# Folding the wide value products: four f32 products with a 0/1 matrix in place of four transposes and a VectorE sum

## The chip, the cores and the metric

The kernel runs on one core of one Trainium2 chip. The metric is the device time of one execution in microseconds (us); lower is better. The kernel before has a median of 193.93 us over 3 runs.

## The reference

One decode step of attention over a sliding window, gated by a small MLP. The inputs are bf16, with 32 heads of 128, a window of the last W = 4096 positions, and x of 512 values:

```
xn = _layernorm(x)
q  = (xn @ wq).reshape(32 heads, 128)
k  = k_cache[:, :, Sk - W:, :]          # 32 x 4096 x 128
v  = v_cache[:, :, Sk - W:, :]          # 32 x 4096 x 128
p  = softmax(einsum("hd,hkd->hk", q, k) * 128 ** -0.5)
s  = einsum("hk,hkd->hd", p, v).reshape(4096) @ wo
g  = silu(mlp(xn))                      # the weights w2, w3 and w4 are used
out = x + s * g
```

K and V of the window are 33.5 MB each. That is most of the 79 MB that one execution reads.

## The kernel before, in words

The 32 heads go in `NG` = 8 groups of `G` = 4 heads. A group's K is one tile of 128 partitions: 32 partitions belong to each head, and each partition holds 128 positions of 128 values (32 KB). The group's V lies in the same way. `load` issues every such load on SyncE's queue, in the order of the program. K tiles come from `k_pool` (3 buffers) and V tiles from `v_pool` (2 buffers), so a load waits on SyncE's queue until the last reader of its buffer is through. The wq load and two small loads of x are issued on ScalarE's queue.

The program begins with constants, the layer norm of x, q and the MLP. The order of instructions on the engines there is left to a planner. Then comes a loop of 10 stages, `for s in range(NG + LAG)` at L531, whose order on TensorE (PE), VectorE (DVE) and ScalarE (ACT) is as written. Stage s works on three groups at once:

- Group s: the scores. VectorE takes half of the positions or more (`k_vector`: a product, L321, and a sum, L323). For the others, TensorE transposes K (`k_turn`, L339), ScalarE copies the result to `kt` (L342), and TensorE multiplies with q (`k_scores`, L350).
- Group s - 1: the softmax. `sm_max` is its maximum on VectorE. `sm_turn` and `sm_exp` bring the maximum of each head to all partitions (L372 to L384) and take the exponentials on ScalarE (L388).
- Group h = s - 2 (`LAG` = 2): the value products. `v_wide` (L427) multiplies four columns of probabilities for four heads at once (16 columns, `pT`) with 512 values of V. So each product holds 4 x 4 blocks of which only those whose column fits the position are wanted, and four row groups at partitions 0, 32, 64 and 96 share the sum. ScalarE copies the result to `ov_sb` (L433), 128 rows of 4 x 128 f32 values.

The wanted rows of `ov_sb` are folded by three steps, one stage later in stages 3 to 6. For block j the wanted row of head a is row 32 r + 4 j + a, for r from 0 to 3, and the four row groups and the four blocks are to be summed:

- `v_turn` transposes the four 128 x 128 blocks on TensorE into one PSUM tile `ot_ps`. Each block is written 4 columns further left than 128 j, so that the wanted columns of all blocks fall in with each other (L444).
- `v_add` sums 16 values for each of the 4 heads on VectorE (L450) and gives `oT`, 128 x 4.
- `v_out` scales `oT` with the inverse denominator `rden`. In groups 0 to 2 that is four ScalarE operations (L475), from group 3 on one VectorE operation (L471).

`ps_misc` is a pool of one PSUM buffer. The tile `ot_ps` of groups 0 to 6, the denominators (`sm_den`, L394, an f32 product of a 128 x 128 matrix of ones with 4 columns, read by `sm_rden` at L399), the transposed maximum, the tile `mb_ps` and the tiles of `ox_pick` follow each other in it. Each waits until the one before has been read. The last group, 7, uses a buffer of `ps_tr`, and its `oT` is a PSUM tile that takes further products (`v_part`) behind the sum.

Groups 0 to 3 are folded in stages 3 to 6, behind `sm_exp` and before `v_wide`. Group 4 is folded early in stage 7, group 5 at the end of stage 7, group 6 in stage 8 and group 7 in stage 9. In stages 8 and 9 the output products with wo (`y_wide`, `y_head`) and a few products on zeros (`warm`) stand between these steps.

Tiles lie in SBUF pool by pool as the program opens them: K, `kt` and `prod`, then constants, small tiles, the softmax's tiles (`sm_pool`), and last the weights, whose place V's tiles take from stage 2 on.

Of the kernel before, what the change touches and what calls it, by code (L numbers as in the profile page):

```python
# [8 lines left out]
P = 128  # L9
BF16 = mybir.dt.bfloat16  # L10
FP32 = mybir.dt.float32
ACT = mybir.ActivationFunctionType
ALU = mybir.AluOpType
AX = mybir.AxisListType
# [4 lines left out]
G = 4  # L19
# [7 lines left out]
def kernel(  # L27
# [14 lines left out]
    nc = tc.nc  # L42
# [20 lines left out]
    const = ctx.enter_context(tc.tile_pool(name="const", bufs=1))  # L63
    small = ctx.enter_context(tc.tile_pool(name="small", bufs=1))
    ps_misc = ctx.enter_context(tc.tile_pool(name="ps_misc", bufs=1, space=PSUM))
    ps_tr = ctx.enter_context(tc.tile_pool(name="ps_tr", bufs=3, space=PSUM))
# [3 lines left out]
    sm_pool = ctx.enter_context(tc.tile_pool(name="sm", bufs=3))  # L70
# [4 lines left out]
    def load(dst, src):  # L75
# [9 lines left out]
                        in_=A_wq.rearrange("(a b c) n -> b a (c n)", a=4, c=KC))  # L85
# [19 lines left out]
    ident_f = const.tile([P, P], FP32, name="ident_f")  # L105
# [16 lines left out]
    nc.vector.memset(neg_half[:], -0.5)  # L122

    masks = {}

# [75 lines left out]
    for b in range(2):  # L203
        zeros(qr[b][:])
        for c in range(KC):
            wc = wq_sb[:, c, :].rearrange("p (g a d) -> p g a d", a=G, d=Dh)
            for a in range(G):
                nc.tensor.matmul(qr[b][32 * a:32 * a + 1], lhsT=xq_bf[:, c:c + 1], rhs=wc[:, 4 * b:4 * b + 4, a, :],  # L208
                                 start=False, stop=(c == KC - 1), skip_group_check=True)
    nc.scalar.copy(out=q_row[:, 0:4, 0, :], in_=qr[0][:])  # L210
    nc.vector.tensor_copy(out=q_row[:, 4:8, 0, :], in_=qr[1][:])  # L211
    for b in range(2):
        qb_ps = ps_tr.tile([P, 4, Dh], FP32, tag="pt", name="qb_ps")
        nc.tensor.matmul(qb_ps[:], lhsT=sel[:].rearrange("k b a -> k (b a)"), rhs=q_row[:, 4 * b:4 * b + 4, 0, :],
                         start=True, stop=True)
        nc.scalar.copy(out=q_bc[:, 4 * b:4 * b + 4, :], in_=qb_ps[:])
    for b in range(2):
# [5 lines left out]
        for t in range(2):  # L223
            rows = slice(64 * t, 64 * t + 64)
            nc.scalar.copy(out=q_pair[rows, 4 * b:4 * b + 4, :, G * t:G * t + G].rearrange("p g l a -> p g a l"),
                           in_=qt_ps[rows].bitcast(BF16).rearrange("p g (a m l) -> p g a m l", a=G, l=2)[:, :, :, 0, :])
# [4 lines left out]
    for j in range(KC):  # L231
        for c in range(KC):
            nc.tensor.matmul(hs_ps[:, j:j + 1], lhsT=w2_sb[:, c, j::4],
                             rhs=shifted_bf[:, c:c + 1], start=(c == 0), stop=(c == KC - 1))
# [33 lines left out]
    for i, (col, w) in enumerate(terms):  # L268
        r = 32 * (i % 4)
        nc.tensor.matmul(hr_ps[r:r + 1].rearrange("r j n -> r (j n)"), lhsT=col, rhs=w, start=False,  # L270
                         stop=(i >= len(terms) - 4), skip_group_check=True)
# [25 lines left out]
                            op=ALU.max)  # L297
# [136 lines left out]

    def v_turn(g):
        s = st[g]
        if g == NG - 1:
            ot_ps = ps_tr.tile([P, 4 * P], FP32, tag="pt", name="ot_ps")
        else:
            ot_ps = ps_misc.tile([P, 4 * P], FP32, tag="misc", name="ot_ps")  # L440
        s["ot"] = ot_ps
        step = P - 4
        for j in range(4):
            nc.tensor.transpose(ot_ps[:, step * j:step * j + P], s["ov_sb"][:, j, :], ident_f[:])  # L444

    def v_add(g):
        s = st[g]
        if g < NG - 1:
            s["oT"] = sm_pool.tile([P, G], FP32, tag="oT", name="oT")
        nc.vector.tensor_reduce(out=s["oT"][:], in_=s["ot"][:].rearrange("p (x m) -> p m x", m=32)[:, 0:G, :],  # L450
                                axis=AX.X, op=ALU.add)

# [72 lines left out]
    NG = H // G  # L525
# [5 lines left out]
    for s in range(NG + LAG):  # L531
# [22 lines left out]
        if s < NG:  # L554
# [11 lines left out]
            if s == 7:  # L566
                v_turn(h - 1)
                v_add(h - 1)
                v_out(h - 1)
            elif s > 1:  # L570
                sm_den(s - 2)
                sm_rden(s - 2)
            elif s == 1:
                sm_max(0)
# [14 lines left out]
            if s == 7:  # L589
                k_vector(s, kn, 2)  # L590
                v_wide(h, v)
                sm_exp(s - 1)
                v_turn(h)
                y_open()
                k_vector(s, kn, 3)
                v_add(h)
                v_out(h)
                ox_spread(1)
                sm_max(s)
                continue  # L600
            if s > 0:
                sm_exp(s - 1)
            if h > 0:
                v_turn(h - 1)
# [3 lines left out]
            if h > 0:  # L608
                v_add(h - 1)
                v_out(h - 1)  # L610
# [74 lines left out]
```

## Time and profile before

| What | Value |
|---|---|
| Median of 3 runs | 193.93 us (193.26 to 193.96) |
| Span of the profiled execution | 191.2 us |
| The profiled execution's own time | not listed beside its span; the median less the span is 2.7 us |
| Busy: PE, DVE, ACT, POOL | 116.4, 150.9, 89.2, 2.3 us |
| DMA | 79.02 MB, mean 413 GB/s over the span |
| Mean granted TensorE clock | 0.720 |
| Four fold transposes of one group (L444) | 0.66 us at granted clock 1.0, 1.05 to 1.11 us at 0.5 |
| The fold's sum (L450) | 8 operations, median 0.215 us |
| Scaling (L471, L475) | 0.16 us each (5), 0.29 us each (12) |

The profile is one execution, and its times count from the span's start. PE is the matmuls, PEld the weight loads. A digit row cuts the span in 40 equal slices of 4.8 us, and each digit is the busy share in tenths. The chain of waits is followed back from the last instruction, at each step to what released it; where it names a DMA, the time runs from the issue of the load to its landing, and waiting in the queue behind earlier loads is part of it. In the windows each line has the stretch, its length, the busy time of the engines with their instruction counts, the granted clock, the mean busy share of the 16 DMA engines and GB/s.

### The profile page before, as it was taken

How to read it: one execution, taken by the hardware profiler on the slowest of the kernel's cores; microseconds unless marked ns; L12 is line 12 of the kernel's file. 1: busy time of each engine (PE TensorE's matmuls, PEld its weight loads, DVE VectorE, ACT ScalarE, POOL GpSimd, SP SyncE). 2: the span in 40 equal slices, each digit the busy share in tenths (PEclk: the TensorE clock that was granted, in tenths of full speed). 3: DMA queues.
4: the chain of work that ended last, by engine and by line, in shares of the span. 5: the costliest groups of instructions: out<-in, count | busy, mean ns of one | idle time of the engine just before them, and what ended most of it. 6: DMA issues, size and time to landing. Idle time of an engine off the chain costs nothing.

```text
span 191.2 us, 2839 instructions
## 1 busy us (share of the span) xinstructions
PE 116.4 (61%) x1159; PEld 74.2 (39%) x1159; DVE 150.9 (79%) x175; ACT 89.2 (47%) x191; POOL 2.3 (1%) x11
## 2 busy tenths in 40 slices
PE   1653754989825368256845772680888189739762
PEld 0430222767614334143334441540763077313322
DVE  1660159979999999999999999999999999980111
ACT  2001370888794076427464564542475148733120
POOL 2110000000000000000000000000000000000000
PEclk9999695555755557955695588557567858975998
DMA  6999999999999999999999999999999998999990
GB/s 211 447 430 404 431 418 439 439 439 437 432 434 439 432 429 432 432 439 432 422 432 432 418 422 418 452 439 435 439 432 434 435 432 372 471 425 405 420 371 32
DMA packets 4572, 79.02 MB, mean 413 GB/s; under 512 B 624, under 2 KB 1232, under 8 KB 1488
## 3 DMA queue, kind: packets, MB, share of 16 engines
q1 hardware_dynamic: 4264, 74.65, 91.6%
q10 hardware_dynamic: 296, 4.20, 5.1%
q8 instruction: 9, 0.15, 0.3%
q14 instruction: 3, 0.02, 0.0%
HBM read 78.84 MB, written 0.00 MB: 412 GB/s over the span
## 4 chain that ended last, share of the span: by engine, by line
DVE 46%; DMA 43%; PE 5%; ACT 3%; issue 1%; SPq 1%; ACTq 0%; DVEq 0%
DMA kv<-in_A_k_cache_dram 31%; DVE S L323 28%; DVE prod L321 15%; DMA kv<-in_A_v_cache_dram 10%; ACT kt L342 3%; DMA x_bf<-in_A_x_dram 2%; PE pt L339 2%; PE ov L427 1%; DVE m L366 1%; DVE S L364 1%; SPq L76 1%; PE sT L350 1%; DVE mx L374 1%; PE oT L461 1%; PE ot_ps L444 0%
## 5 line engine op out<-in xcount | busy, mean ns | idle before, releaser
L323 DVE TENSOR_REDUCE S<-prod 128x20 f32<-128x2560 bf16 (+1 forms) x32 | 86.0, 2686 | 1.1
L342 ACT COPY kt<-pt 128x1024 bf16<-128x1024 bf16 x52 | 51.2, 1013 | 40.4 <-PE pt L339 38.7
L339 PE MATMUL pt<-ident_f,kv 128*128 128x128 f32 x208 | 46.7, 376 | 10.8 <-DMA kv<-in_A_k_cache_dram 10.8
L321 DVE TENSOR_TENSOR prod<-kv,q_bc 128x2560 bf16<-128x2560 bf16 (+1 forms) x32 | 45.4, 1418 | 3.9 <-DMA kv<-in_A_k_cache_dram 3.7
L339 PEld LDWEIGHTS pt<-ident_f,kv 128*128 128x128 f32 x208 | 34.2, 196 | 14.4 <-DMA kv<-in_A_k_cache_dram 10.5
L350 PE MATMUL sT<-q_pair,kt 128*128 128x8 bf16 x416 | 19.4, 170 | 15.7 <-ACT kt L342 15.5
L350 PEld LDWEIGHTS <-kt 128*128 128x128 bf16 x416 | 16.4, 104 | 26.8 <-ACT kt L342 25.8
L427 PE MATMUL ov<-kv,pT 128*16 128x512 bf16 x248 | 22.0, 515 | 1.4 <-DMA kv<-in_A_v_cache_dram 1.4
L388 ACT ACTIVATE pT<-S,mb 128x128 bf16<-128x128 f32 x32 | 13.9, 573 | 0.3
L372 PE MATMUL mt_ps<-ident_f,m 128*1 128x128 f32 x8 | 2.9, 359 | 17.4 <-DVE rden L399 16.9
L433 ACT COPY ov_sb<-ov 128x512 f32<-128x512 f32 x8 | 4.7, 586 | 17.1 <-PE ov L427 17.1
L427 PEld LDWEIGHTS <-pT 128*16 128x16 bf16 x248 | 6.9, 109 | 13.2 <-issue 11.4
L359 ACT ACTIVATE own<-sT,par 128x48 f32<-128x48 f32 (+1 forms) x32 | 7.5, 356 | 3.7 <-PE sT L350 3.7
L444 PE MATMUL ot_ps<-ident_f,ov_sb 128*128 128x128 f32 x32 | 7.1, 359 | 2.9 <-ACT mb L384 1.9
L211 DVE CAST q_row<-qr_ps 128x512 bf16<-128x512 f32 x1 | 0.7, 692 | 9.9 <-PE qr_ps L208 9.9
L388 ACT ACTIVATION_READ_ACCUMULATOR pT<-S,mb 128x1 f32 x32 | 8.3, 258 | 0.0
L372 PEld LDWEIGHTS mt_ps<-ident_f,m 128*1 128x1 f32 x8 | 0.6, 80 | 17.9 <-DVE rden L399 17.2
L399 DVE RECIPROCAL rden<-den_ps 128x4 f32<-128x4 f32 x8 | 1.4, 175 | 7.0 <-PE den_ps L394 7.0
L381 PE MATMUL mb_ps<-md,par_t 5*128 5x4 f32 x16 | 3.9, 311 | 4.1 <-DVE md L376 4.1
L255 ACT ACTIVATE a_row<-a_ps 128x384 bf16<-128x384 f32 x1 | 0.5, 491 | 12.0 <-remote 12.0
L444 PEld LDWEIGHTS ot_ps<-ident_f,ov_sb 128*128 128x128 f32 x32 | 4.5, 178 | 3.9 <-ACT mb L384 2.3
L208 PE MATMUL qr_ps<-wq_sb,xq_bf 128*1 128x512 bf16 x32 | 3.1, 566 | 3.7 <-DMA wq_sb<-in_A_wq_dram 3.7
(122 smaller groups left out, 81.6 us busy)
## 6 DMA issues: line engine op xcount, KB each, us to landing
kv<-in_A_k_cache_dram SPq DMA_DIRECT2D x7, 4096.0 KB, 31.3
kv<-in_A_v_cache_dram SPq DMA_DIRECT2D x7, 4096.0 KB, 30.6
wq_sb<-in_A_wq_dram ACTq DMA_DIRECT2D x1, 4096.0 KB, 17.6
kv<-in_A_k_cache_dram SPq DMA_DIRECT2D x2, 2048.0 KB, 27.4
wo<-in_A_wo_dram SPq DMA_DIRECT2D x1, 2048.0 KB
kv<-in_A_v_cache_dram SPq DMA_DIRECT2D x1, 2048.0 KB
kv<-in_A_v_cache_dram SPq DMA_DIRECT2D x2, 1024.0 KB, 17.6
w_sb<-in_B_w_dram SPq DMA_DIRECT2D x1, 1376.0 KB, 9.1
```

What stands on the lines that cost most here:

```text
L321: nc.vector.tensor_tensor(out=prod[:, 0:m, :], in0=kn[:, rows, :], in1=q_bc[:, g:g + 1, :].to_broadcast([P, m, Dh]), op=ALU.mult)
L323: nc.vector.tensor_reduce(out=st[g]["S"][:, rows], in_=prod[:, 0:m, :], axis=AX.X, op=ALU.add)
L339: nc.tensor.transpose(pt[:, i, :], kn[:, c:c + 2, :].rearrange("p c d -> p (c d)").bitcast(FP32), ident_f[:])
L342: nc.scalar.copy(out=kts[b][:, 0:n, :], in_=pt[:, 0:n, :].bitcast(BF16))
L350: nc.tensor.matmul(st[g]["sT"][:, c:c + 2, :].rearrange("p c a -> p (c a)"), lhsT=kt[:, i, l::2], rhs=q_pair[:, g, l, :], start=(l == 0), ...
L359: nc.scalar.mul(s["own"][:, 0:m, a], s["sT"][:, 0:m, a], par[:, a:a + 1])
L372: nc.tensor.transpose(mt_ps[:], s["m1"][:], ident_f[:])
L381: nc.tensor.matmul(mb_ps[:], lhsT=par_t[:].rearrange("k b a -> k (b a)"), rhs=md[:], start=True, stop=True)
L388: nc.scalar.activation(out=s["pT"][:, :, a], in_=s["S"][:], func=ACT.Exp, scale=scale, bias=mb[:, a:a + 1], accum_out=s["sum"][:, a:a + 1])
L427: nc.tensor.matmul(ov[r:r + 4 * G], lhsT=s["pT"][:, c:c + 4, :].rearrange("p i a -> p (i a)"), rhs=v[:, c:c + 4, :], start=(i < 4), stop=( ...
L433: nc.scalar.copy(out=s["ov_sb"][:], in_=ov[:])
L444: nc.tensor.transpose(ot_ps[:, step * j:step * j + P], s["ov_sb"][:, j, :], ident_f[:])
```

## The change

A constant `fold` (128 x 4 x 4, f32) is made of the identity by one VectorE maximum: for block j and head a, it has ones in the four rows 32 r + 4 j + a. In groups 0 to 6, `v_turn` multiplies each block of `ov_sb`, as the stationary operand, with that block's 4 columns of `fold`, and the four products add up in one PSUM tile `oT` of 128 x 4 in the pool `ps_misc`. `v_add` does nothing there any more, and `v_out` reads `oT` from PSUM where it read SBUF. Group 7 is left as it was. The SBUF tiles `oT` of `sm_pool` (three buffers of 16 bytes per partition, each in a slot of 32) go away, and `fold` takes 64 bytes per partition.

```diff
+    fold = const.tile([P, 4, G], FP32, name="fold")
+    nc.vector.tensor_reduce(out=fold[:].rearrange("p j a -> p (j a)"),
+                            in_=ident_f[:].rearrange("p (r m) -> p m r", m=32)[:, 0:4 * G, :],
+                            axis=AX.X, op=ALU.max)
...
     def v_turn(g):
         s = st[g]
-        if g == NG - 1:
-            ot_ps = ps_tr.tile([P, 4 * P], FP32, tag="pt", name="ot_ps")
-        else:
-            ot_ps = ps_misc.tile([P, 4 * P], FP32, tag="misc", name="ot_ps")
+        if g < NG - 1:
+            s["oT"] = ps_misc.tile([P, G], FP32, tag="misc", name="oT")
+            for j in range(4):
+                nc.tensor.matmul(s["oT"][:], lhsT=s["ov_sb"][:, j, :], rhs=fold[:, j, :], start=(j == 0),
+                                 stop=(j == 3))
+            return
+        ot_ps = ps_tr.tile([P, 4 * P], FP32, tag="pt", name="ot_ps")
         s["ot"] = ot_ps
         step = P - 4
         for j in range(4):
...
     def v_add(g):
         s = st[g]
         if g < NG - 1:
-            s["oT"] = sm_pool.tile([P, G], FP32, tag="oT", name="oT")
+            return
         nc.vector.tensor_reduce(out=s["oT"][:], in_=s["ot"][:].rearrange("p (x m) -> p m x", m=32)[:, 0:G, :],
                                 axis=AX.X, op=ALU.add)
```

## The prediction

> **What bounds the kernel now.** I read the page's totals and slices first, then the chain of waits, then the DMA issues, and last the windows, to see whether the chain tells the truth.
>
> ```profile
> span 191.2 us, 2839 instructions
> ...
> DVE  1660159979999999999999999999999999980111
> ...
> DMA  6999999999999999999999999999999998999990
> ```
>
> Two resources are full from about 30 to 165 us: VectorE and the DMA engines. Only DMA stays full from 2 to 186 us. Which one sets the end decides everything, because the change takes work from VectorE and adds none to DMA.
>
> ```profile
> 128.66 0.13 DVE oT L450
> 128.79 1.41 DVE prod L321
> 130.20 0.02 SPq L76
> 130.22 0.03 issue
> 130.25 23.26 DMA kv<-in_A_k_cache_dram
> 153.52 0.04 issue
> 153.56 1.13 PE pt L339 x4
> ...
> 167.79 18.54 DMA kv<-in_A_v_cache_dram
> 186.33 0.05 issue
> 186.38 0.97 PE oT L461 x32
> ```
>
> The chain names VectorE up to 130 us, with the reduction that the change removes (L450) on it. But it jumps into loads of 23.26 and 18.54 us. A 4096 KB load (4.19 MB) takes 9.7 us at the 432 GB/s of the windows below. So the K load issued at 130.25 lay 23.26 - 9.7 = 13.6 us behind earlier loads. An issue a little earlier or later lands at the same time.
>
> ```profile
> kv<-in_A_k_cache_dram SPq DMA_DIRECT2D x1, 4096.0 KB, 22.1
> ```
>
> ```profile
> 60.45:78.65 18.20, 10.28 (x109) 6.55 (x109) 17.98 (x13) 9.56 (x21) 0.00 (x0) 0.64 1.01 433
> 78.65:96.87 18.22, 10.62 (x96) 6.74 (x97) 18.02 (x14) 8.00 (x22) 0.00 (x0) 0.63 1.00 431
> ...
> 153.50:170.30 16.80, 12.92 (x143) 9.33 (x143) 16.06 (x21) 11.19 (x22) 0.00 (x0) 0.80 1.01 435
> 170.30:186.40 16.10, 11.85 (x116) 4.85 (x117) 2.63 (x13) 3.67 (x12) 0.00 (x0) 0.82 0.96 402
> 186.40:191.20 4.80, 1.33 (x48) 1.05 (x48) 0.75 (x3) 0.00 (x0) 0.00 (x0) 0.85 0.09 32
> ```
>
> The first line is the DMA issue at 112.03 us, the shortest wait of any full K or V load: 22.1 - 9.7 = 12.4 us of queue ahead of it. The others range up to 38.3 us. The windows (columns: PE, PEld, DVE, ACT, POOL busy, granted clock, DMA share, GB/s) show a DMA share of 1.0 in stages where VectorE is busy 99% too, and 0.96 in the stage after 170 us where VectorE has almost nothing to do (2.63 of 16.1 us). The page counts 79.02 MB; at 432 GB/s that is 183 us of the 191.2. The rest is the start, and the 4.8 us behind the last landing at 186.4 us. The kernel is bound by its loads.
>
> The sum is made against a time. Span 191.2 us, median of the runs 193.93, so about 2.7 us lie around the span (2.1 to 2.8 over the three runs).
>
> **The change part by part.** *VectorE loses* seven reductions of 0.215 us (the tile's row gives 215/215/233 ns for all eight; the eighth stays): 1.5 us busy. On the chain each shows as 0.13 us, since its start overlaps the tail of the operation before it; around 147.4 and 157.5 us the step to the next start is 0.25 us. So between 0.9 and 1.75 us leave VectorE's order. In stages 3 to 6 the next K load is issued up to that much earlier in all, into a queue at least 12.4 us deep: worth 0.
>
> *VectorE gains* the reduction that makes `fold`, 64 values in and 16 out per partition: between 0.215 us (L450, also 64 values) and 0.37 us (L296, 128 values). It needs only the identity matrix, ready at 1.8 us, and VectorE stands idle 3.4 us before 4.7 us and 9.87 us before 23.1 us. Even in the worst place, ahead of the q chain, 0.37 us is covered: TensorE waits until 19.9 us for wq. Without that cover it would cost 0.37 us.
>
> *TensorE.* A 0/1 product in f32 is not in the trace, but the denominator's product has the same stationary size and the same 4 columns, and it runs as two weight loads and two matmuls (x16 for eight calls).
>
> ```profile
> 88.92 1.11 PE L444 MATMUL ot_ps<-ident_f,ov_sb 128*128 128x128 f32 x4 [0.25 <-ACT mb L384]
> ```
>
> ```profile
> 173.22 0.50 PEld L394 LDWEIGHTS den_ps<-sum,ones_f 128*128 128x128 f32 x2 [0.85 <-ACT mb L384]
> 173.23 0.59 PE L394 MATMUL den_ps<-sum,ones_f 128*128 128x4 f32 x2
> 178.40 0.39 PE L394 MATMUL den_ps<-sum,ones_f 128*128 128x4 f32 x2
> ```
>
> Four transposes last 1.11 us at the granted clock of 0.5 and 0.66 us at 1.0. A pair of denominator passes takes 0.59 us at 0.5; one lasts 0.376, so a pass follows the last after 0.21 us. At 1.0 I take 0.36 to 0.39 us for a pair and 0.25 for one: 0.11 us apart. Eight passes are then 7 x 0.21 + 0.38 = 1.85 us or 7 x 0.11 + 0.25 = 1.02 us. That is +0.74 us in groups 0, 1, 2 and 4 (clock 0.5) and +0.36 us in groups 3, 5 and 6 (1.0), about 4 us of TensorE over the kernel. Bounds for one group: nothing (if the passes overlap fully) to twice the transposes, +1.1 us. In stages 3 to 6 this delays the wide products, and so the release of a V buffer and a V load's issue, by 0.4 to 1.1 us; those loads take 25.9 to 32.3 us to land, 9.7 of them transfer, so it is hidden by 16 us.
>
> The rows have an f32 weight load at 186 to 190 ns at the full clock and up to 333 at half, 0.11 or 0.21 us from the next. The Trainium skill ("TensorE: Matmul & The Clock Gate", LDWEIGHTS) gives a load its column count over 1.2 in ns, 107 for 128 columns, whatever the clock. By it, an estimate, eight passes would end after some 1.1 us in every group, so the groups at half clock would pay nothing and stage 7 would not slip. The trace's 0.21 us contradicts it at half clock; either way the time comes to 193.9, as the cost is hidden.
>
> Stage 7 is tightest: there the chain runs on TensorE from 153.5 to 166.5 us, and the last V load is issued behind its wide product. Group 4's +0.74 us moves that issue (166.8 to 167.8 us) to at most 168.9. V's last 4.19 MB and the last 0.52 MB of wo rows need 10.9 us and end at about 186.4, so they start at about 175.5: 6 us or more are left. In stage 8, group 6 ends 0.36 us later, but its 0.25 us step on VectorE is gone. The warm products behind it end at 180.5, the first V piece lets TensorE go on at 181.5, and the second at 183.9: a delay of 0.36 to 1.1 us is taken up there. Behind 186.4 us nothing is changed.
>
> *Waits.* The product now stays in the one `misc` bank until the output scaling has read it. In groups 0 to 2 that is ScalarE (four operations, 0.85 us from 94.09), so the next user, the denominator's product at 96.10, waits for ScalarE in place of VectorE. It stands behind scores that wait for a `kt` copy, which ScalarE issues after those four operations: nothing added. From group 3 VectorE's scaling reads PSUM; its row is 161/164/164 ns, group 7's from PSUM among them: 0.
>
> Sum: 193.93 - 0 (VectorE) + 0 (TensorE) = **193.9 us**.
>
> **The rivals.** *Loads into shifted tiles get dearer (slower).* `fold` adds 64 bytes per partition ahead of the pools of weights and V; `oT` frees three slots of 32. Laid out in order, those tiles start 32 bytes lower, so no longer at a multiple of 64. K tiles lie in front and keep their place. The moved tiles take some 42 MB (V 33.6, wq and w2 to w4 7.5, wo 1.0), or 97.5 us of transfer. One extra 256-byte piece per 32 KB row would be 1/128: 0.76 us, 194.7. One extra 32-byte step for each 256 bytes would be 1/8: 12 us, 206. It decides (over 0.97 us) from 1% per moved byte, and there is no queue to hide it. For it: DMA has no slack. Against it: K tiles and V tiles already lie differently against 256 bytes, and they stream alike.
>
> ```profile
> q1 hardware_dynamic: 126, 3.64, 99.8%
> ```
>
> ```profile
> q1 hardware_dynamic: 116, 3.44, 99.6%
> ```
>
> First a window inside the K load that lands at 153.5 (144.5 to 153 us), then one inside the V load that lands at 143.8 (135 to 143 us): 3.64 / (8.5 x 16 x 0.998) and 3.44 / (8 x 16 x 0.996), 26.8 and 27.0 GB/s per engine. No load of size here starts 32 bytes off, so the trace doesn't exclude it. The Trainium skill ("DMA: Bandwidth & Descriptors", How a descriptor splits into AXI transactions) says that a descriptor whose start is off a multiple of 256 bytes pays for one more transaction: the 0.76 us case. K against V shows no such price. Chance 0.27, most of it between 194.9 and 198.
>
> *VectorE is the bound after all (faster).* The chain's 46% speaks for it, the queue of 12 us against it. It gives 193.93 less 0.9 to 1.75: 192.2 to 193.0. Chance 0.05.
>
> *The last V load starves (slower).* If the DMA queue ran dry before it, stage 7's +0.74 and group 6's +0.36 us would come through: 195.0. It needs a delay of over 6 us. Chance 0.04.
>
> **How the numbers follow.** The forecast has 0.64; its own range is 193.2 to 194.5. About 0.5% (0.97 us) is what a measurement of this kernel can tell from no change; the three runs spread over 0.70 us. Slower by more: 0.23 of the first rival and 0.04 of the last, 0.27. Faster by more: 0.05, and 0.02 for spread. Within: 0.66. The range takes the forecast, the edge of the faster case and the shifted-tile case up to 2% per moved byte and some more: 193.0 to 197.0.
>
> **What would show it.** Right: DMA still 9 in every slice to the end, 32 KB rows at the same pace, the last V landing near 186.4, L450 once, some 16 TensorE passes for each of groups 0 to 6 (8 loads, 8 matmuls) in 1.0 to 1.9 us, and a tail of 4.8 us. Wrong: V windows below K windows in GB/s (tiles), an earlier last landing (VectorE), a gap in DMA before the last V load (starving), or TensorE at a lower granted clock behind 186 us.

## The result and the profile after

The changed kernel takes 195.44 us (median of 4 runs, 195.36 to 195.51) against 193.63 us for the kernel before in the same job: 1.0102 times, 95% interval 1.0089 to 1.0116. It is slower by 1.8 us, inside the range, and not where the forecast put it. Two small costs on the loads make the difference, both side effects of where the change put bytes and instructions: one 16 KB instruction fetch that now comes ahead of the last V rows, and tiles that no longer start at a multiple of 256 bytes.

The profiled run took 195.36 us with a span of 193.6. First the lines of its page that answer to those of before:

```profile
span 193.6 us, 2890 instructions
...
PE 124.7 (64%) x1187; PEld 82.4 (43%) x1187; DVE 150.3 (78%) x169; ACT 89.0 (46%) x191; POOL 2.3 (1%) x11
...
DVE  1660069979999999999999999998999986970111
...
DMA  6999999999999999999999999999999998998960
```

TensorE has 28 more weight loads and 28 more matmuls (1187 against 1159): four more of each in every one of the seven groups. DMA still stands at 8 or 9 until shortly before the end. The end has moved, though. In the chain of waits (start, length, what):

```profile
130.49 23.37 DMA kv<-in_A_k_cache_dram
...
170.35 18.14 DMA kv<-in_A_v_cache_dram
188.49 0.05 issue
188.54 0.97 PE oT L469 x32
```

The last V piece lands at 188.49 us, where before it was 186.33: 2.16 us later. Its issue came 2.56 us later, at 170.35, and that is not the reason: in e3 below, which has no new fold, it is issued at 170.35 too and lands at 187.04:

```profile
170.35 16.70 DMA kv<-in_A_v_cache_dram
```

The windows (PE, PEld, DVE, ACT, POOL busy, granted clock, DMA share, GB/s):

```profile
60.45:78.65 18.20, 9.98 (x109) 6.53 (x109) 17.96 (x14) 9.79 (x21) 0.00 (x0) 0.65 1.01 431
...
173.00:188.50 15.50, 12.24 (x118) 5.05 (x118) 1.61 (x9) 3.57 (x12) 0.00 (x0) 0.80 0.88 359
188.50:193.60 5.10, 1.58 (x48) 1.16 (x48) 0.74 (x3) 0.00 (x0) 0.00 (x0) 0.59 0.01 4
```

In mid-kernel the DMA engines are as busy and move a little less, 431 GB/s where it was 433. In the stage up to V's landing they are busy 0.88 on average, where it was 0.96: most have finished while the chain still waits for V, and the packet records below show that one of the 16 is late. The answer to which transfer made it late is in the DMA queues between 5 and 186 us, first of the kernel before, then of the changed one (queue, packets, MB, share):

```profile
q8 instruction: 8, 0.13, 0.3%
```

```profile
q8 instruction: 9, 0.15, 0.3%
```

Queue q8 brings 16 KB of instructions at a time. Nine such packets stand in each trace. The ninth came at 187.05 us before, behind V's last row, and at 185.58 us after, ahead of it. The packet records show its price: the fetch took its engine 1.10 us, and the V row of 8 KB behind it 0.77 us where such a row takes 0.31. That is 1.10 and another 0.46 us on one engine. Its last V rows ended at 187.44, 187.75 and 188.06 us; every other V row had ended by 186.49, 1.57 us earlier.

### The profile page after: what moved, and what is told of

It is laid out like the page before. It is cut to its first block, busy times and chain, and to the rows that moved or that the text cites. A ratio compares the mean times of both kernels' runs of the same rounds, so it can differ in the third digit from the quotient of the medians.

```text
span 193.6 us, 2890 instructions
## 1 busy us (share of the span) xinstructions
PE 124.7 (64%) x1187; PEld 82.4 (43%) x1187; DVE 150.3 (78%) x169; ACT 89.0 (46%) x191; POOL 2.3 (1%) x11
## 4 chain that ended last, share of the span: by engine, by line
DVE 43%; DMA 42%; PE 10%; ACT 2%; issue 1%; SPq 1%; ACTq 0%; DVEq 0%
DMA kv<-in_A_k_cache_dram 31%; DVE S L328 26%; DVE prod L326 13%; DMA kv<-in_A_v_cache_dram 9%; PE pt L344 3%; PE ov L432 3%; DMA x_bf<-in_A_x_dram 2%; PE oT L445 2%; ACT kt L347 2%; PE sT L355 1%; DVE m L371 1%; DVE S L369 1%; SPq L76 1%; DVE mx L379 1%; PE oT L469 1%
## 5 line engine op out<-in xcount | busy, mean ns | idle before, releaser
L344 PE MATMUL pt<-ident_f,kv 128*128 128x128 f32 x208 | 48.8, 389 | 9.8 <-DMA kv<-in_A_k_cache_dram 9.8
L344 PEld LDWEIGHTS pt<-ident_f,kv 128*128 128x128 f32 x208 | 35.8, 203 | 13.1 <-DMA kv<-in_A_k_cache_dram 9.4
L432 PE MATMUL ov<-kv,pT 128*16 128x512 bf16 x248 | 22.7, 528 | 0.0
L445 PE MATMUL oT<-fold,ov_sb 128*128 128x4 f32 x56 | 10.8, 317 | 1.9 <-ACT mb L389 1.5
L445 PEld LDWEIGHTS oT<-fold,ov_sb 128*128 128x128 f32 x56 | 10.2, 274 | 2.4 <-ACT mb L389 2.0
L213 PE MATMUL qr_ps<-wq_sb,xq_bf 128*1 128x512 bf16 x32 | 3.6, 627 | 3.9 <-DMA wq_sb<-in_A_wq_dram 3.9
```

Of the source, the lines that this page charges most:

```text
L344: nc.tensor.transpose(pt[:, i, :], kn[:, c:c + 2, :].rearrange("p c d -> p (c d)").bitcast(FP32), ident_f[:])
L432: nc.tensor.matmul(ov[r:r + 4 * G], lhsT=s["pT"][:, c:c + 4, :].rearrange("p i a -> p (i a)"), rhs=v[:, c:c + 4, :], start=(i < 4), stop=( ...
L445: nc.tensor.matmul(s["oT"][:], lhsT=s["ov_sb"][:, j, :], rhs=fold[:, j, :], start=(j == 0), stop=(j == 3))
```

## The experiments

All times are medians, with the ratio to the kernel before in the same job. The end of V's rows is read from the packet records of each profile: where the last rows follow each other by 0.31 us, the time of one row, they are one engine's. The two columns on V's rows carry the argument:

```
                         fetches     all other     the late     time,    ratio to before
                         before      V rows        engine's     us       (95% interval)
                         186 us      ended by      last V row
before                   8           185.93        -            193.4 to 193.6
after                    9           186.49        188.06       195.44   1.0102 (1.0089-1.0116)
e1 40 pairs              9           185.89        187.12       194.86   1.0078 (1.0059-1.0097)
e2 after, tiles back     9           185.77        187.21       194.39   1.0055 (1.0035-1.0076)
e3 tiles 32 down         8           186.57        -            194.37   1.0048 (1.0033-1.0064)
e4 bf16 fold, tiles back 8           185.89        -            193.32   0.9995 (0.9979-1.0012)
e5 12 pairs              8           186.06        -            193.27   0.9991 (0.9982-1.0000)
e6 100 pairs             9           186.03        187.25       194.77   1.0067 (1.0053-1.0081)
e7 tiles 64 down         8           186.62        -            194.19   1.0039 (1.0026-1.0052)
e8 tiles 128 down        8           186.39        -            194.18   1.0038 (1.0026-1.0051)
e9 fold in 0 to 2        8           185.89        -            193.30   0.9995 (0.9984-1.0006)
e10 K and V at 256       8           185.40        -            193.19   0.9994 (0.9984-1.0005)
e11 K at 256, V at 128   8           185.84        -            193.64   1.0012 (1.0003-1.0021)
e12 40 pairs, 32 down    9           186.65        188.14       196.12   1.0144 (1.0129-1.0159)
```

**Taking the two causes apart.** e1 gives the kernel before more TensorE instructions and nothing else:

```diff
     region.__enter__()
+    for _ in range(40):
+        nc.tensor.matmul(ov[:, 0, 0:4], lhsT=zero_bf[:], rhs=zero_bf[:, 0:4], start=True, stop=True,
+                         skip_group_check=True)
```

> Kernel before with 40 more tiny TensorE products on zeros ahead of the loop (40 weight loads and 40 matmuls), where TensorE is idle; tiles, folds and VectorE untouched. Instruction-fetch theory: in the changed kernel the last 16 KB fetch of TensorE's instructions (queue q8) came at 185.6 us, before the last V row had landed, and in the kernel before at 187.1, behind it; each fetch costs its DMA engine about 1.6 us, and V's end waits for the slowest engine. With 40 pairs more the last fetch comes before 186 us: about 1.2 to 1.7 us slower than before, 194.9 to 195.3, one engine's last V rows 1 to 1.6 us behind the others'. Shifted-tile theory: tiles have not moved, no change, 193.6. TensorE-delay theory (folds in stage 7 delay the last V load): no change, 193.6.

194.86 us. Every fetch comes earlier (the seventh at 147.6 us instead of 150.0, the ninth at 182.9 instead of 187.1), so q8 follows TensorE's instruction count. The last V rows of one engine end 1.23 us behind all others.

e2 takes the tile shift out of the changed kernel, e3 puts it alone into the kernel before. `pad` is an unused tile ahead of the pools of weights and V:

```diff
-    small.tile([P, 96], BF16, name="pad")
+    small.tile([P, 112], BF16, name="pad")     # e2, on the changed kernel: V at a multiple of 256 again
+    small.tile([P, 80], BF16, name="pad")      # e3, on the kernel before: 32 bytes lower
```

> Changed kernel with the unused tile pad 32 bytes longer, so that weights and V start at a multiple of 256 bytes again as before. Shifted-tile theory as the whole cause: 193.6, no slower than before. Instruction-fetch theory with a small tile share: V rows of 32 KB go back from 1216 to 1224 ns to 1213, worth 0.4 to 0.6 us, the rest stays: 194.8 to 195.1. TensorE-delay theory: 195.4 as the changed kernel.

> Kernel before with the unused tile pad 32 bytes shorter, so that weights and V start 32 bytes lower as in the changed kernel; no instruction changed. Shifted-tile theory as the whole cause: 195.4. Instruction-fetch theory with a small tile share: V rows at 1216 to 1224 ns, +0.4 to +0.6 us, 194.0 to 194.2, unless the later end lets the last fetch in ahead of V's end, then about 195. TensorE-delay theory: 193.6.

194.39 and 194.37 us: each keeps about half. e2 has the late engine and V rows at 1213 ns; e3 has no late engine and all V rows 0.64 us later. The excess over before in each is 0.55% and 0.48%, together 1.03%; the change has 1.02%. TensorE's folds don't end e2's chain either: its last V load is issued at 169.74 us, earlier than e3's, and lands at 187.64, 0.60 us later than e3's, and TensorE waits 0.94 us for it. Whether f32 folds cost something by themselves is tried, for three groups, in e9.

e4 keeps the new folds but in bf16, one weight load and one matmul each, as many instructions as the transposes had:

```diff
-    fold = const.tile([P, 4, G], FP32, name="fold")
+    fold = const.tile([P, 4, G], BF16, name="fold")
...
-        s["ov_sb"] = sm_pool.tile([P, 4, Dh], FP32, tag="ov_sb", bufs=2, name="ov_sb")
+        # groups 0 to 6: the same tile in BF16, tag "ov_h"; pad 128 long, so V at a multiple of 256
```

> Changed kernel with the copy of the wide products and the 0/1 matrix in bf16 for groups 0 to 6 (rounds the wide sums to bf16; each fold product is then one weight load and one matmul, so TensorE has as many instructions as before the change), tiles back at a multiple of 256 bytes. Instruction-fetch theory: the last fetch falls behind V's end again, 193.4 to 193.8. Shifted-tile theory: 193.6. TensorE-delay theory: the folds get shorter than the transposes, 193.6 or less. VectorE theory: if its seven saved sums are worth anything it shows here, 192.2 to 193.0.

193.32 us, 0.9995 (0.9979 to 1.0012): both costs gone, and nothing gained from VectorE's seven sums. Its runs spread more than the others', from 192.77 to 194.29 us. In the profiled one, of 194.07, TensorE starts the last V products at 187.13 us without waiting for their load, though the V rows had ended by 185.89: once the loads are in time, TensorE isn't far behind them.

**How the fetch costs.** e5 and e6 change the count of e1's loop to 12 and 100.

> As e1, with 12 more TensorE pairs on zeros in place of 40. Instruction-fetch theory: the last fetch moves 12 pairs forward, to 186.5 us or later, still behind V's last row: no change, 193.3 to 193.8. If it were the additional TensorE work or instructions themselves that cost: 0.3 of e1's 1.3 us, 193.9.

> As e1, with 100 more TensorE pairs on zeros. The ninth fetch (the one that came at 182.9 us in e1) then comes at about 175 us, and the tenth after the end. Theory that the ninth fetch meets an engine that has had one already and that no engine can catch up: as e1, 194.6 to 195.2, one engine's last V rows 1.2 to 1.6 us behind. Theory that a fetch costs only when it falls among the last rows: 193.5. Theory that the instructions themselves cost: 2.5 times e1's 1.3 us, 196.9.

193.27 us and 194.77 us. So neither the instructions nor their work cost anything: 12 pairs are free and 100 cost no more than 40. Queue q8 between 5 and 186 us, e5 and then e6:

```profile
q8 instruction: 8, 0.13, 0.3%
```

```profile
q8 instruction: 9, 0.15, 0.3%
```

The step is the ninth fetch. In e6 it comes at 176.0 us, 10 us ahead of the end, and the engine that it met is 1.2 us late at the end all the same: with every engine full, none catches up. The eighth fetch, at 175.3 us before, costs nothing visible. The packet records don't name the engines, but each load ends with 16 records of 4 bytes, one for each engine, and their spread tells which engines are behind. Before, after one, four, six and eight fetches (at 39.6, 97.8, 141.4 and 179.0 us), just one, four, six and eight of the 16 end the load 1.55 to 1.99 us behind the first of them. (Two more stand between at 179.0 us, at 1.17 and 1.50; they fell back behind the three 8 KB instruction packets of queue q14.) So the first eight fetches met eight different engines, and the loads, which end with their slowest engine, paid for little more than the first. The ninth met an engine that was behind already, in the changed kernel as in e1, e2, e6 and e12: its last V rows end 1.2 to 1.6 us after those of all other engines, also of those with one fetch. In e1 that engine's rows, each of which starts where the one ahead ends, lead back to the only engine that was behind at 41 us, the one that met the first fetch; in the other four the records allow the same and don't force it. That suggests a round of eight engines.

e9 uses the change itself for the dose: the f32 folds in groups 0 to 2 alone, 12 pairs instead of 28, tiles back.

```diff
     def v_turn(g):
-        if g < NG - 1:
+        if g < 3:
...
     def v_add(g):
         s = st[g]
-        if g < NG - 1:
+        if g < 3:
```

(Groups 3 to 6 have the transposes and the sum of the kernel before again, and `pad` is 64 long.)

> Changed kernel with the f32 fold products in groups 0 to 2 alone (groups 3 to 6 keep transposes and the VectorE sum), tiles back at a multiple of 256 bytes. It adds 12 TensorE pairs in place of 28, so the last instruction fetch stays behind V's last row, as in e5. Instruction-fetch theory: no change, 193.2 to 193.7, although three groups fold in the new way. If the f32 products cost by themselves: 3/7 of e2's 0.87 us, 193.9. VectorE theory: 3 x 0.13 us less, 193.1.

193.30 us, as e5. Three groups folded in the new way cost nothing.

**How the tiles cost.** e7 and e8 shorten `pad` by 64 and 128 bytes. e10 puts 128 bytes ahead of the K tiles (with `pad` 128 shorter), e11 does only the first.

> Kernel before with the unused tile pad 64 bytes shorter: weights and V start at a multiple of 64 bytes, 64 short of a multiple of 256 (192 past one). If the price of e3 comes from not starting at a multiple of 64: V rows at 1213 ns, 193.5. If from not starting at a multiple of 128 or 256: V rows at 1216 to 1224 ns again, 194.2 to 194.5.

> Kernel before with pad 128 bytes shorter: weights and V start 128 past a multiple of 256, where the K tiles start. As K's rows in the kernel before (1213 ns, a few at 1218 to 1221): 193.5 to 193.7. By the rule that a row off a multiple of 256 pays for one more transaction: as e3, 194.2 to 194.5.

> Kernel before with 128 unused bytes ahead of the K tiles and the unused tile pad 128 bytes shorter: K tiles now start at a multiple of 256 bytes too, weights and V as before. If each row pays for its own start off 256: the K rows' 1214 to 1224 ns go to 1213, 193.0 to 193.4. If only the weights' and V's place matters: 193.5.

> Kernel before with 128 unused bytes ahead of the K tiles: K tiles start at a multiple of 256 bytes, weights and V 128 past one. If each row pays for its own start: V's and the weights' rows pay as in e8, K's nothing, 193.8 to 194.0. If it is the weights' and V's place alone, whatever K's: 194.2 as e8.

e7 and e8 pay 0.69 and 0.68 us, so it is 256 bytes that counts, not 64 or 128. But e11 pays only 0.26 us (1.0012) although V, at 128, is off, and not on its loads: its V rows end at 185.84 us, no later than before. The packet records show why (mean ns of a 32 KB row inside one load, rows that share an engine with a fetch left out; K2 follows K1, K6 follows the first wo block, which lies in a K buffer; the others follow a load of the other kind):

```
            K start  V start   K2       K5       K6       V4       V5
before      128      0         1217.3   1213.9   1217.4   1213.0   1213.0
after       128      224       1217.3   1217.4   1216.6   1218.3   1218.1
e3          128      224       1219.9   1217.4   1217.2   1218.2   1218.0
e8          128      128       1217.1   1217.6   1216.7   1217.9   1217.2
e10         0        0         1213.0   1213.0   1213.0   1213.0   1213.0
e11         0        128       1213.0   1213.0   1213.0   1213.3   1213.7
```

(Starts are bytes past a multiple of 256, as the program places the tiles.) A load off 256 runs at full pace if the load ahead of it on the queue was on 256, and pays some 4 to 5 ns per row, 0.4%, if that one was off too. Before, every second load was V's, on 256, so only K1 (1217.5 ns, behind the two pieces of group 0's K), K2 and K6 paid. The shift took that away from all of them: 0.4% of some 140 us of K and V is 0.5 to 0.6 us, and e3's rows end 0.64 us later. Why the second one pays was not tried.

**Both at once, and the way on.** e12 puts e1 and e3 together, without touching a fold.

> Kernel before with e1's 40 TensorE pairs on zeros and e3's pad 32 bytes shorter; folds untouched. If the two causes add up and nothing else matters: 193.5 + 1.3 + 0.85, 195.4 to 195.8, the changed kernel's time without any change to the folds. If the late fetch and the shifted rows share one cost: 194.9.

196.12 us, over the change's 195.44 and over the sum of e1 and e3 (1.0144 against 1.0126, 0.35 us). Here the fetch comes at 183.5 us, two V pieces ahead of the end instead of one as in the changed kernel, so the late engine delays the second piece as well. In e1, with its fetch at 182.9, it does so too. TensorE's timeline, of e12, of e1 and then of the changed kernel:

```profile
186.15 0.61 PE L427 MATMUL ov<-kv,pT 128*16 128x512 bf16 x8 [1.98 <-DMA kv<-in_A_v_cache_dram]
187.44 1.11 PE L444 MATMUL ot_ps<-ident_f,ov_sb 128*128 128x128 f32 x4 [0.69 <-ACT ov_sb L433]
```

```profile
185.15 0.61 PE L427 MATMUL ov<-kv,pT 128*16 128x512 bf16 x8 [1.79 <-DMA kv<-in_A_v_cache_dram]
186.44 0.68 PE L444 MATMUL ot_ps<-ident_f,ov_sb 128*128 128x128 f32 x4 [0.69 <-ACT ov_sb L433]
187.59 1.01 PE L461 MATMUL oT<-pT,kv 128*128 128x4 bf16 x32
```

```profile
185.02 0.60 PE L432 MATMUL ov<-kv,pT 128*16 128x512 bf16 x8
186.37 0.66 PE L452 MATMUL ot_ps<-ident_f,ov_sb 128*128 128x128 f32 x4 [0.75 <-ACT ov_sb L438]
188.54 0.96 PE L469 MATMUL oT<-pT,kv 128*128 128x4 bf16 x32 [1.19 <-DMA kv<-in_A_v_cache_dram]
```

In e12 the second piece's products wait until 186.15, in e1 until 185.15. In both, TensorE then starts the last V products without waiting for their load, so TensorE is on the path. In e12 it also runs the transposes of the last group at half clock (1.11 us against 0.68), about as much as the excess over the sum. In the changed kernel that piece was in time.

e10's V rows end 0.53 us earlier than before and the time stays at 193.19 (0.9994). In its profile the last V products start at 186.27 us behind the transposes and the `y_sum` products, not behind the landing. e13 (e10) and e14 (before) put those products behind the last V products:

```diff
-            rows_add(y_ps, ind, y_sum, False)
             v_part(h, v, cuts[2], CP)
+            rows_add(y_ps, ind, y_sum, False)
```

> e10 (K, weights and V at a multiple of 256 bytes) with the y_sum products of the last stage moved behind the last V products on TensorE. If TensorE's order sets the end once the loads end earlier: 0.3 to 0.5 us less than e10, 192.7 to 193.0, the last V products starting at V's landing, near 185.9 us. If the time around the span or the granted clock swallows it: 193.2 as e10.

> Kernel before with the same reorder alone. There the last V products start at V's landing (186.4 us) and TensorE stood idle 0.2 us ahead of them, so the moved products only leave the wait and go in ahead of the output products, where TensorE waits 0.26 us for VectorE: no change to 0.15 us slower, 193.4 to 193.6.

e13: in the profiled run, of 192.99 us, the last V products start at the landing again, at 185.82, but the median is 193.22, 0.9992 (0.9976 to 1.0008), and the 0.3 to 0.5 us forecast for it don't show. e14: 193.52, 1.0001 (0.9990 to 1.0012). No version here is measurably faster than the kernel before.

## Why the prediction was right and wrong

**Right: what bounds the kernel.** The loads do. VectorE's saved sums are worth nothing in time: e4 saves all seven and e9 three, and both stand at 0.9995.

**Right: the sizes on the engines.** Eight passes were to take 1.85 us at half clock and 1.02 us at full. The changed kernel's TensorE timeline, groups 4 and 6:

```profile
156.35 1.85 PE L445 MATMUL oT<-fold,ov_sb 128*128 128x4 f32 x8
```

```profile
181.49 1.05 PE L445 MATMUL oT<-fold,ov_sb 128*128 128x4 f32 x8 [0.38 <-ACT ov_sb L438]
```

The seven groups took 10.8 us in place of 6.4, so 4.4 us more where about 4 were forecast. The row of the tile also settles what was weighed there: the Trainium skill ("TensorE: Matmul & The Clock Gate", LDWEIGHTS) gives a load its columns over 1.2 in ns, 107 for 128, and the f32 loads here took 186 to 333.

```profile
L445 PEld LDWEIGHTS oT<-fold,ov_sb x56: 186/333/333, 89.2 to 182.3; 128*128 128x128 f32 x56
```

`fold` itself took 0.26 us at 7.64 us, hidden. L450's operation is left once, in group 7.

**Right: the last V load doesn't starve.** Its issue slipped further than the 168.9 us allowed for it, to 170.35, and the queue still covered that, as e3's equal issue and earlier landing show. e3 has no new fold, so the folds alone don't explain the slip; the granted clock between 153.5 and 170.3 us was 0.64 after, 0.75 in e3 and 0.80 before.

**Wrong: "+ 0 (TensorE)".** The step counted TensorE's time and found cover for it. It didn't count its instructions. It rests on the premise that the change "adds none to DMA", and that is what failed: 28 pairs more bring the ninth instruction fetch ahead of V's end, on the one resource that has no cover, and the sum has no term for it. That is about half of the loss: 1.57 us on the late engine, 0.87 us of time in e2.

**Wrong: the reading behind the shifted-tile rival.** It was given 0.27 and left out of the sum, and it happened, as the other half: 0.85 us in e3. That this is close to its low end of 0.76 is luck. The 0.76 is 1/128 of the time of the moved tiles, 9.5 ns for a row of 1213; a row paid about half of that, and K's rows, which hadn't moved, paid too. So its own sign, V windows below K windows, hardly showed either (rows of 1218 against 1217 ns). What failed is the evidence held against it, that K and V windows stream alike. K's rows were off 256 and cheap only because V's were on, and the K window that was compared lies in K7, behind a V load. K1, K2 and K6, the K loads behind another load that was off, carried the price in the trace of before (1217 ns against 1213). The Trainium skill ("DMA: Bandwidth & Descriptors", How a descriptor splits into AXI transactions) gives a descriptor that starts off a multiple of 256 bytes one more transaction; it says so of what a transaction reads, and here the tiles that are written moved. e7 and e8 agree on the 256; e11 disagrees that each such row pays.

**Wrong in part: "behind 186.4 us nothing is changed".** The instructions are the same, but the stretch from V's landing to the end grew from 4.85 to 5.08 us. TensorE had waited 1.19 us for the late rows, and its granted clock there was 0.59 (0.85 before): the last 16 products took 0.62 us instead of 0.39. After, then before:

```profile
189.75 0.62 PE L160 MATMUL y_ps<-wo_rows,o 128*1 128x128 bf16 x16 [0.26 <-DVE o L479]
```

```profile
187.59 0.39 PE L155 MATMUL y_ps<-wo_rows,o 128*1 128x128 bf16 x16 [0.26 <-DVE o L471]
```

That the wait lowered the clock isn't shown: in e8 TensorE waits 0.22 us there, and these products take 0.60.

**Not settled.** The span grew by 2.4 us and the time by 1.8. What lies around the span was 1.8 us in every run of the changed kernel, 1.7 to 1.9 in e2 and e4, 2.0 to 2.2 in e9, and 2.1 to 2.3 in all other kernels, the one before included (the prediction's 2.7 set one profile's span against the median of other runs). So this time shrinks with the number of groups folded in the new way, and no run tells why. With it, e2's span is 1.3 us longer than before and its time 0.87.

## What to carry to other kernels

When a kernel is bound by its loads, cost an edit by what it does to the DMA engines, even if it moves no load: how many instructions it adds (they are fetched by the same engines, 16 KB at a time) and where it leaves the tiles that the loads fill. Look up in the trace when the fetches come, and how far each engine is behind when a load ends: a fetch is free on an engine that is ahead and costs on the one that is last. A pad tile that keeps load tiles at a multiple of 256 bytes is cheap, and it is to be set again after every edit that adds or frees a tile.

## What the runs showed of the hardware that was not expected

- TensorE's instructions came in nine packets of 16,384 bytes in this kernel, one for about 130 of its 1159 weight-load and matmul pairs. One such fetch among full queues put its DMA engine 1.57 us behind, though 16 KB of data, half a row of 1.21 us, take an engine 0.61 us. The Trainium skill ("Runtime: NRT & Kernel Launch", Terms) says that an engine's instruction memory is refilled in 16 KiB blocks; the traces agree.
- The first eight fetches met eight different DMA engines (in the kernel before, eight of 16 are 1.56 to 1.99 us behind at 179 us), and the ninth, in all five kernels where it came ahead of V's end, one that was behind already.
- A delay of one DMA engine stayed with it for 10 us of full queue (e6) and delayed the whole load, which ends with its slowest engine.
- Loads off 256 bytes cost 0.4% only behind another such load in these runs: rows of 1217 to 1218 ns against 1213, with V at 128 free behind K at 0 (e11) and dear behind K at 128 (e8).
